# Token-sum stores in the feed-forward, the surplus branch two steps earlier, and feed-forward weight loads ahead of the last outputs

## The chip, the cores and the metric

The kernel runs on one core of one Trainium2 chip, as one launch. The metric is the device time of an execution in microseconds (us). The engines are TensorE (PE, matmul; PEld its weight loads), VectorE (DVE), ScalarE (ACT), GpSimd (POOL) and SyncE (SP, which here issues nearly all DMAs). Each engine runs its own instructions in order and waits for others through semaphores.

## The reference

```python
# retention: 8 batches x 8 heads, 576 positions, head width 64
ret = (q @ k.transpose(0, 1, 3, 2)) / sqrt(64) * Dmat   # Dmat[h,i,j] = gamma_h**(i-j), 0 where j > i
x = (ret @ v) laid out as 4608 tokens x 512
# top-1 mixture of 8 experts
logits = x @ w_gate + modality_bias[modality_id]
e = argmax(logits); gate = softmax(logits)[e]
x = gate * (relu(x @ w1[e]) @ w2[e])                    # 512 -> 1024 -> 512
# dense feed-forward
h = relu(x @ w_in)                                      # 512 -> 2048
out = (h * h) @ w_out                                   # 2048 -> 512
```

All inputs and the output are fp32. The kernel computes each product with fp32 accuracy from a high and a low part of both operands: three matmuls, high by high, high by low and low by high.

## The kernel before, in words

**Stages.** `phase0` computes the retention and the routing. `phase12` (line 664) runs the experts over sorted slots of tokens: a first slot "E", then slots 0 to 8 (`NF` is 8, the last one, 256 tokens wide, the others 512). `phase3` (line 1087) runs the dense feed-forward over nine tiles of 512 tokens, three passes over 3, 3 and 2 blocks of the hidden width. Intermediate data lie in device memory: `yd` the experts' outputs, `sd` the token numbers of the sorted order, `wc` the feed-forward weights in sums and split, `xc` the token sums of a tile, `pd` partial outputs.

**A slot.** Each slot has eight steps f = 0 to 7. A step is `first` (the first product, 12 matmuls per step, relu into hh and hl by ACT and DVE) and `second` (12 matmuls that add to four banks). The first of step f+1 is written ahead of the second of step f. The weights of two steps come as two raw loads `wr` (`wload`, line 400, three buffers) that ACT and DVE split into high and low (lines 149 and 150). At f = 7, `second` copies the slot's result to ye, stores it to yd (line 834) and stores the token numbers to sd (line 835, pieces of 4 bytes).

**Side work of the last slots.** `combos` (lines 745 to 781) reads tile 0 of yd (line 750), makes the seven token sums that the feed-forward's seven-product scheme wants, in tiles x0 to x3 that stay for the feed-forward, and stores each to xc (line 762). `wload2` (line 1008, the load is line 1012) loads one feed-forward weight block, two tiles of 917 KB: w00, w01, w02 are the first product's three blocks, w10, w11, w12 those of the second, each with 0 and 1 for high and low. `extras` (line 922) holds the blocks for surplus tokens under a branch (line 904); with these inputs none is taken, so every engine only jumps over it.

**The order of the feed-forward.** A planner (`Plan`, line 1020) takes all operations of phase 3 with a cost on each engine and what they read and write, and places them in a list schedule by start and due time; the code is emitted in that order. `xprep` (line 1151) loads a tile's yr from yd, makes the seven sums x0 to x3 (two per tile), and stores them to xc. `one` is the first product of a block with its relu and square into z and split into h; `two` is the second product into oe. All DMAs of phase 3 are issued by SP at line 1129, in the planner's order.

Of the kernel before, what the change touches and what calls it, by code (L numbers as in the profile page):

```python
# [88 lines left out]
def kernel(ctx, tc, qT, kT, kN, vN, modT, w_gate, mbias, w1, w2, w_in, w_out,  # L89
# [574 lines left out]
    def phase12():  # L664
        with ExitStack() as c1:
# [79 lines left out]
            def combos():  # L745
                for _ in cs:
                    pass
                yr = cv.tile([P, KD, TS], F32, tag="w", name="eyr")
                tx = cv.tile([P, 2, 256], F32, tag="w", name="etx")
                sp.dma_start(yr, yd[:, 0:TS].rearrange("(c p) t -> p c t", p=P))  # L750
                yield 1
                xs = [cv.tile([P, 2, 2, 2, 256], F32R, tag="w", name=f"x{a}") for a in range(4)]
                b11, b12 = yr[:, 0:2, 0:256], yr[:, 0:2, 256:512]
                b21, b22 = yr[:, 2:4, 0:256], yr[:, 2:4, 256:512]

                def sub(o, a, b):
                    dve.tensor_tensor(out=o, in0=a, in1=b, op=ALU.subtract)

                def put(m, src):
                    t_ = held["x", m] = xs[m // 2][:, m % 2]  # L760
                    split(t_[:, 0], t_[:, 1], src, dve)
                    sp.dma_start(xc[0, m], t_.bitcast(F32).rearrange("p a k t -> p (a k t)"))

                sub(tx, b12, b11)
                put(0, b11)
                yield 1
                put(1, b21)
                yield 1
                sub(b12, b22, b12)
                put(2, b22)  # L770
                yield 1
                sub(b11, b22, tx)
                put(3, tx)
                yield 1
                put(5, b12)
                yield 1
                sub(b21, b21, b11)
                put(4, b11)
                yield 1
                put(6, b21)  # L780
                yield 1
# [28 lines left out]
            def second(u, cols=range(KD)):  # L810
                s, f = u
                wd = width(s)
                hh, hl = HS.pop(u)
                w = W[s, f // 2][1]
                for c in cols:
                    if f == 0:
                        Y[s, c] = new(psY, [P, TS], F32, f"y{c}", f"y{c}")
                    cs = slice(c * P, c * P + P)
                    three(Y[s, c][:, :wd], (w[:, 0, f % 2, cs], w[:, 1, f % 2, cs]), (hh, hl), f == 0, f == 7)
                if f == 7:  # L820
                    if 0 in cols:
                        YE[s] = new(rp, [P, KD, TS], F32, "raw", "ye")
                    ye = YE[s]
                    for c in cols:
                        act.activation(ye[:, c, :wd], Y[s, c][:, :wd], AF.Copy)
                    if 3 not in cols:
                        return
                    ix = XG[s][1]
                    if s == "E":
                        yo, so = yd[:, 0:TS], sd[0:TS]  # L830
                    else:
                        reg = sp.value_load(slots[0:1, 2, s:s + 1], min_val=0, max_val=NT)
                        yo, so = yd[:, bass.ds(reg, wd)], sd[bass.ds(reg, wd)]
                    sp.dma_start(yo.rearrange("(c p) t -> p c t", p=P), ye[:, :, :wd])
                    sp.dma_start(so.rearrange("(j p) -> p j", p=P), ix[:, :wd // P])
# [113 lines left out]
            for i, u in enumerate(us):  # L949
                s, f = u  # L950
                k = seq.index(s)
                nx = seq[k + 1] if k + 1 < len(seq) else None
                if nx is not None and f == (4 if s == "E" else 0):
                    gather(nx)
                if i + 1 < len(us):
                    first(us[i + 1])
                if nx is not None:
                    if s == "E" and f == 6:
                        trans(nx, 0)
                        trans(nx, 1)  # L960
                    elif s != "E" and 3 <= f <= 6:
                        trans(nx, f - 3)
                if u == (NF, 7):
                    wload2(1, 0, wp)
                second(u)
                if s == "E" and f == 6:
                    trans(nx, 2)
                    trans(nx, 3)
                if i == 2:
                    route_c(last)  # L970
                if i == 0:
                    for _ in route_a(last):
                        pass
                elif i == 1:
                    tb = table()
                    next(tb)
                    for _ in route_b(last, dve):
                        next(tb)
                elif i == 2:
                    ws(6, 2, 7)  # L980
                    tab_out()
                    for _ in range(10):
                        next(tb)
                elif i == 3:
                    for _ in tb:
                        pass
                    ws(8, 2, 11)
                else:
                    wl(i + 9)
                    fill(wsg(i + 6, 2 if i < 10 else 1, i + 9), part(cs, 2250))  # L990
                    if i >= 68:
                        run(ex, 3)
                    if i == 73:
                        assert next(cs, 0) == 0 and next(ex, 0) == 0
                        wload2(0, 0, cv)
                if u == (NF, 1):
                    wload2(0, 1, wp)
                if u == (NF, 4):
                    extras()
                if u == (NF, 5):  # L1000
                    wload2(0, 2, wp)
                if i == 6:
                    ext = nc.values_load(slots[0:1, 3, 0:1], min_val=0, max_val=NX)
            assert st["ld"] == st["sp"] == nw
# [82 lines left out]
    def phase3():  # L1087
        with ExitStack() as c2:
            ff = c2.enter_context(tc.tile_pool(name="ff", bufs=1))
            sb = lambda name, shape, dt=F32R: ff.tile(shape, dt, tag=name, name=name)  # L1090
            plan = Plan()
            for j in (1, 2):
                wload2(1, j, wp, False)
            WT = [[[held["w", m, j, x] for x in range(2)] for j in range(3)] for m in range(2)]
            XT = [held["x", m] for m in range(7)]
            HT = [sb(f"h{j}", [P, 2, 7, 256]) for j in range(3)]
# [31 lines left out]
            def dma(o, i, kb, r, w, early=False):  # L1128
                plan.add(m_(kb), lambda e: (pool if early else e).dma_start(o, i), r, w, 2.0)
# [21 lines left out]
            def xprep(n):  # L1151
                p, t = T3[n]
                if n == 0 or T3[n - 1][1] == t:
                    return
                if p:
                    for x in AT1:
                        m = MX[x]
                        dma(XT[m].bitcast(F32).rearrange("p a k t -> p (a k t)"), xc[t, m], 512, [("xc", t, m)],
                            [("x", m, 0), ("x", m, 1)])
                    return  # L1160
                for a in range(2):
                    dma(yr[:, 2 * a:2 * a + 2],
                        yd[2 * a * P:2 * a * P + 2 * P, t * TS:t * TS + TS].rearrange("(c p) t -> p c t", p=P),
                        512, [], [("b", a, 0), ("b", a, 1)])
                b11, b12 = yr[:, 0:2, 0:256], yr[:, 0:2, 256:512]
                b21, b22 = yr[:, 2:4, 0:256], yr[:, 2:4, 256:512]
                k11, k12, k21, k22 = ("b", 0, 0), ("b", 0, 1), ("b", 1, 0), ("b", 1, 1)
                def put(x, src, k):
                    m = MX[x]
                    hilo(XT[m][:, 0], XT[m][:, 1], src, 512, [k], ("x", m, 0), ("x", m, 1))  # L1170
                    dma(xc[t, m], XT[m].bitcast(F32).rearrange("p a k t -> p (a k t)"), 512,
                        [("x", m, 0), ("x", m, 1)], [("xc", t, m)])

                sub = ALU.subtract
                tt(xt, b12, b11, sub, 512, [k12, k11], [("t",)], p_(512))
                tt(b12, b22, b12, sub, 512, [k22, k12], [k12], p_(512))
                put(1, b11, k11)
                tt(b11, b22, xt, sub, 512, [k22, ("t",)], [k11], p_(512))
                put(2, b21, k21)
                tt(b21, b21, b11, sub, 512, [k21, k11], [k21], p_(512))  # L1180
                put(6, b11, k11)
                put(5, xt, ("t",))
                put(7, b12, k12)
                put(4, b21, k21)
                put(3, b22, k22)
# [115 lines left out]
            for n in range(9, len(T3)):  # L1301
                VO.append(VO[-1] if T3[n][1] == T3[n - 1][1] else 1 - VO[-1])
            plan.add([(DMA_, 8.0)], lambda e: None)
            loadw(0, 1, 1)
            for n, (p, t) in enumerate(T3):
                nq = len(PASSES[p])
                order = sorted((7 * q + AT1[x], q, x) for q in range(nq) for x in AT1)
# [53 lines left out]
```

## Time and profile before

| | us |
|---|---|
| median of 3 runs | 1434.08 (1429.42 to 1436.12) |
| the profiled execution's own time | 1428.05 |
| its span in the trace | 1426.3 |
| TensorE busy in the span | 1358.7 (95%) |
| VectorE, ScalarE, GpSimd busy | 1026.4 (72%), 635.8 (45%), 172.6 (12%) |
| mean granted TensorE clock | 0.984 |

The experts end and the feed-forward begins at about 661 us of the span. An entry such as `PE L787 MATMUL bank<-hh,wy` is a TensorE instruction of line 787 that reads hh and wy and writes a PSUM bank; `[4.96 <-ACT hh L803]` says that the engine was idle for 4.96 us before it, and that ACT's writing of hh at line 803 ended this. A `q` behind an engine's name (SPq, DVEq) is its instruction queue. PEclk is the clock that was granted to TensorE, as a share of full speed.

### The profile page before, as it was taken

The numbers are of one execution on the slowest core, as the hardware profiler recorded it, in microseconds if no ns is written. First come the engines' busy times: TensorE is split into PE (matmuls) and PEld (weight loads), VectorE is DVE, ScalarE is ACT, GpSimd is POOL, SyncE is SP. The second block draws the span as 40 slices with busy tenths as digits, with TensorE's granted clock in tenths as the row PEclk, the third lists the DMA queues.
The fourth block names the chain that finished last, engine by engine and source line by source line (L and its number), as shares of the span: only waits on it lengthen the run. The fifth ranks groups of instructions, "written<-read, shape, count | busy, mean of one in ns | idle before, by whom it ended". The sixth has DMA issues, their size and how long they took to land. (4 is left out here: it accounts for less than half of the span.)

```text
span 1426.3 us, 26456 instructions
## 1 busy us (share of the span) xinstructions
PE 1358.7 (95%) x10384; PEld 1251.9 (88%) x10384; DVE 1026.4 (72%) x2004; ACT 635.8 (45%) x1317; POOL 172.6 (12%) x164
## 2 busy tenths in 40 slices
PE   6999998999999999988899999999999999999985
PEld 6898877888788888878899999999999999999984
DVE  2677756887878878553888887767766777688764
ACT  1444543545354454443555555554434444334321
POOL 3222112101110110000211111100000000021112
PEclk9999999999999999998999999999999999999998
DMA  9978256888889888888644455477445564787672
GB/s 341 355 271 296 78 167 229 246 237 254 298 244 269 251 318 229 236 235 272 234 178 178 185 215 194 179 312 265 174 163 195 211 224 184 276 278 274 222 252 102
DMA packets 143733, 332.40 MB, mean 233 GB/s; under 512 B 20208, under 2 KB 54512, under 8 KB 143600
## 3 DMA queue, kind: packets, MB, share of 16 engines
q1 hardware_dynamic: 135520, 310.06, 64.9%
q0 software_dynamic: 5920, 19.40, 3.6%
q8 instruction: 83, 1.36, 0.4%
q10 hardware_dynamic: 2160, 1.17, 0.3%
q14 instruction: 50, 0.41, 0.1%
HBM read 222.57 MB, written 108.02 MB: 232 GB/s over the span
## 5 line engine op out<-in xcount | busy, mean ns | idle before, releaser
L1140 PE MATMUL bank<-w,h 128*128 128x256 f32 x1008 | 284.8, 283 | 9.4 <-DVE h L1241 9.4
L1138 PE MATMUL bank<-w,h 128*128 128x256 f32 x1008 | 283.9, 282 | 7.8 <-DVE oe L1116 7.7
L1138 PE MATMUL bank<-x,w 128*128 128x256 f32 x1008 | 285.8, 284 | 1.4 <-DVE z L1116 0.9
L1139 PE MATMUL bank<-x,w 128*128 128x256 f32 x1008 | 285.7, 283 | 1.5 <-DVE x L1116 1.5
L1140 PE MATMUL bank<-x,w 128*128 128x256 f32 x1008 | 285.4, 283 | 0.1
L1139 PE MATMUL bank<-w,h 128*128 128x256 f32 x1008 | 283.3, 281 | 1.2 <-DMA w<-wc 1.2
L1113 ACT ACTIVATE z<-bank 128x256 f32<-128x256 f32 x288 | 109.1, 380 | 277.2 <-PE bank L1140 258.4
L1140 PEld LDWEIGHTS bank<-w,h 128*128 128x128 f32 x1008 | 190.3, 189 | 12.2 <-DVE h L1241 11.9
L1138 PEld LDWEIGHTS bank<-w,h 128*128 128x128 f32 x1008 | 191.0, 189 | 9.3 <-DVE oe L1116 8.2
L1139 PEld LDWEIGHTS bank<-x,w 128*128 128x128 f32 x1008 | 193.1, 192 | 2.1 <-DVE x L1116 2.1
L1138 PEld LDWEIGHTS bank<-x,w 128*128 128x128 f32 x1008 | 192.7, 191 | 1.8 <-DVE z L1116 1.1
L1140 PEld LDWEIGHTS bank<-x,w 128*128 128x128 f32 x1008 | 193.2, 192 | 0.4 <-DMA w<-wc 0.4
L1139 PEld LDWEIGHTS bank<-w,h 128*128 128x128 f32 x1008 | 190.3, 189 | 1.4 <-DMA w<-wc 1.4
L1240 ACT ACTIVATE h<-z 128x512 fp32r<-128x512 f32 (+2 forms) x270 | 158.1, 599 | 68.4 <-DVE z L1116 46.5
L1241 DVE TENSOR_TENSOR h<-z,h 128x512 fp32r<-128x512 f32 (+2 forms) x270 | 173.8, 672 | 3.7 <-ACT h L1240 3.7
L1116 DVE TENSOR_TENSOR z<-z,bank 128x256 f32<-128x256 f32 x216 | 89.7, 418 | 58.8 <-PE bank L1140 53.4
L787 PE MATMUL bank<-hh,wy 128*128 128x512 f32 (+1 forms) x320 | 127.0, 397 | 5.0 <-ACT hh L803 5.0
L787 PE MATMUL bank<-xh,wx 128*128 128x512 f32 (+1 forms) x320 | 124.5, 389 | 3.4 <-PEq L904 3.4
L788 PE MATMUL bank<-xl,wx 128*128 128x512 f32 (+1 forms) x320 | 124.3, 388 | 1.1 <-DVE xl L743 1.1
L788 PE MATMUL bank<-hl,wy 128*128 128x512 f32 (+1 forms) x320 | 124.4, 389 | 0.7 <-DVE hl L804 0.7
L1116 DVE TENSOR_TENSOR z<-z 128x256 f32<-128x256 f32 x288 | 121.8, 451 | 3.1
L789 PE MATMUL bank<-xh,wx 128*128 128x512 f32 (+1 forms) x320 | 123.9, 387 | 0.0
(168 smaller groups left out, 2223.4 us busy)
## 6 DMA issues: line engine op xcount, KB each, us to landing
x<-xc SPq DMA_DIRECT2D x112, 512.0 KB
wr<-w SPq DMA_DIRECT2D x80, 512.0 KB
xc<-x SPq DMA_DIRECT2D x63, 512.0 KB
w<-wc SPq DMA_DIRECT2D x32, 896.0 KB
wc<-cwh SPq DMA_DIRECT2D x16, 896.0 KB
wc<-cwl SPq DMA_DIRECT2D x16, 896.0 KB
pd<-oe SPq DMA_DIRECT2D x24, 512.0 KB
xd<-xs SPq DMA_DIRECT2D x9, 1024.0 KB
```

The source lines that it names most:

```text
L787: pe.matmul(ps, lh, rh, start=first, stop=False)
L788: pe.matmul(ps, lh, rl, start=False, stop=False)
L789: pe.matmul(ps, ll, rh, start=False, stop=last)
L1113: plan.add(a_(c), lambda e: e.activation(o, i, f), r, w)
L1116: plan.add(engs or d_(c), lambda e: e.tensor_tensor(out=o, in0=a, in1=b, op=op), r, w)
L1138: e.matmul(ps[n], lh, rh, start=first and n == 0, stop=False, skip_group_check=True)
L1139: e.matmul(ps[n], lh, rl, start=False, stop=False, skip_group_check=True)
L1140: e.matmul(ps[n], ll, rh, start=False, stop=True, skip_group_check=True)
L1240: plan.add(a_(c), lambda e: e.activation(h[:, 0, a:b], z[:, a + 1:b + 1], AF.Copy), rs, ks[0])
L1241: plan.add(d_(c), lambda e: e.tensor_tensor(out=h[:, 1, a:b], in0=z[:, a + 1:b + 1], in1=h[:, 0, a:b].bitcast(F32), op=ALU.subtract), rs + ...
```

## The change

The store of each token sum is taken out of `combos`; `xprep` issues those seven stores of tile 0 ahead of tile 1's loads, in an order that the planner chooses. `extras` moves from behind step 4 of the last slot to behind step 2. The load of w02 moves from step 5 to step 3, that of w10 from step 7 to step 4; w11 is loaded at step 5, and w12 inside the `second` of step 7, ahead of the stores to yd and sd. Before, w11 and w12 were loaded by the planner's code.

```diff
@@ combos @@
                     split(t_[:, 0], t_[:, 1], src, dve)
-                    sp.dma_start(xc[0, m], t_.bitcast(F32).rearrange("p a k t -> p (a k t)"))
@@ second, f == 7 @@
                     ix = XG[s][1]
+                    if s == NF:
+                        wload2(1, 2, wp)
                     if s == "E":
@@ the loop over steps @@
-                if u == (NF, 7):
-                    wload2(1, 0, wp)
                 second(u)
...
                 if u == (NF, 1):
                     wload2(0, 1, wp)
-                if u == (NF, 4):
+                if u == (NF, 2):
                     extras()
-                if u == (NF, 5):
-                    wload2(0, 2, wp)
+                for f_, m, j in ((3, 0, 2), (4, 1, 0), (5, 1, 1)):
+                    if u == (NF, f_):
+                        wload2(m, j, wp)
@@ phase3 @@
-            for j in (1, 2):
-                wload2(1, j, wp, False)
@@ xprep @@
+                if n == 1:
+                    for m in range(7):
+                        dma(xc[0, m], XT[m].bitcast(F32).rearrange("p a k t -> p (a k t)"), 512,
+                            [("x", m, 0), ("x", m, 1)], [("xc", 0, m)])
                 for a in range(2):
@@ phase3 @@
-            loadw(0, 1, 1)
             for n, (p, t) in enumerate(T3):
```

On VectorE in the last expert slot the rows ahead of the branch were these (wx and wy are split weight blocks, hl the low part of a step's hidden values):

```order
L804 SCALAR_TENSOR_TENSOR hl_5961<-bank7_91,hh_5960 128x256
L150 TENSOR_TENSOR wy_5976<-wr2_5876,wy_5976 128x1024
L804 SCALAR_TENSOR_TENSOR hl_5992<-bank5_89,hh_5991 128x256
L804 SCALAR_TENSOR_TENSOR hl_6020<-bank6_90,hh_6019 128x256
L904 COMPARE_AND_BRANCH
```

and are now:

```order
L150 TENSOR_TENSOR wx_5930<-wr1_5815,wx_5930 128x1024
L803 SCALAR_TENSOR_TENSOR hl_5954<-bank7_91,hh_5953 128x256
L150 TENSOR_TENSOR wy_5969<-wr2_5869,wy_5969 128x1024
L905 COMPARE_AND_BRANCH
```

Two hl have moved behind the branch, and the split of the last wy stands right ahead of it.

On SyncE at the end of that slot (w020 is the first of the two tiles of w02, and so on) it was:

```order
L1012 DMA w020_9090<-wc_95 128x1792
L1012 DMA w021_9092<-wc_95 128x1792
L1012 DMA w100_9122<-wc_95 128x1792
L1012 DMA w101_9124<-wc_95 128x1792
L832 TENSOR_LOAD slots_100
L832 ISA x2
L834 REGISTER_ALU
L834 DMA yd_93<-ye_9138 128x4x256
L835 REGISTER_ALU
L835 DMA sd_94<-ix_5525 128x2x1
L1129 DMA w110_9163<-wc_95 128x1792
L1129 DMA w111_9164<-wc_95 128x1792
```

and from w101 on it is now:

```order
L1012 DMA w110_9091<-wc_95 128x1792
L1012 DMA w111_9093<-wc_95 128x1792
L1012 DMA w120_9140<-wc_95 128x1792
L1012 DMA w121_9142<-wc_95 128x1792
L833 TENSOR_LOAD slots_100
L833 ISA x2
L835 REGISTER_ALU
L835 DMA yd_93<-ye_9135 128x4x256
L836 REGISTER_ALU
L836 DMA sd_94<-ix_5525 128x2x1
L1127 DMA xc_97<-x0_5726 128x1024
L1127 DMA yr_9170<-yd_93 128x2x512
```

The four loads of w11 and w12 now stand ahead of the stores to yd and sd, and a store to xc stands between these and the first load of yr.

On ScalarE in the first feed-forward tile (z and h of the three blocks, x0 of tile 1, oe the output) the rows were:

```order
L1113 ACTIVATE z2_9172<-bank5_89 128x256
L1121 ACTIVATE z1_9171<-z1_9171 128x256
L1122 ACTIVATE z1_9171<-z1_9171 128x256
L1240 ACTIVATE h2_9169<-z2_9172 128x512
```

and are now:

```order
L1111 ACTIVATE z2_9169<-bank5_89 128x256
L1111 ACTIVATE x0_5726<-yr_9170 128x512
L1119 ACTIVATE z1_9168<-z1_9168 128x256
L1120 ACTIVATE z1_9168<-z1_9168 128x256
L1242 ACTIVATE h2_9166<-z2_9169 128x512
```

The copy of x0 out of yr, which stood behind the first copy to oe, now stands inside the last block's z and h work.

## Rows read from the trace of the kernel before

**Rows 1.** Timeline of TensorE, last expert slot: start, duration, instruction, [idle before, its releaser].

```profile
634.74 0.28 PE L787 MATMUL bank<-xh,wx 128*128 128x256 f32 x1
644.12 0.58 PE L787 MATMUL bank<-hh,wy 128*128 128x256 f32 x1 [4.96 <-ACT hh L803]
645.44 0.58 PE L788 MATMUL bank<-hl,wy 128*128 128x256 f32 x1 [0.74 <-DVE hl L804]
651.57 0.55 PE L787 MATMUL bank<-xh,wx 128*128 128x256 f32 x1 [3.42 <-PEq L904]
661.41 0.28 PE L1138 MATMUL bank<-x,w 128*128 128x256 f32 x1
```

**Rows 2.** Windows; columns: length, busy (count) of PE, PEld, DVE, ACT, POOL, PEclk, DMA share, GB/s.

```profile
632.00:640.00 8.00, 7.16 (x61) 6.95 (x59) 1.65 (x2) 0.46 (x2) 0.00 (x0) 1.00 1.08 149
652.00:657.00 5.00, 5.00 (x25) 5.00 (x25) 0.42 (x1) 0.38 (x1) 0.00 (x0) 0.50 0.57 217
```

**Rows 3.** Timeline of ScalarE, three loads that it waited for.

```profile
411.50 1.06 ACT L149 ACTIVATE wy<-wr 128x1024 fp32r<-128x1024 f32 x1 [3.43 <-DMA wr<-w]
614.97 0.63 ACT L149 ACTIVATE x<-eyr 128x512 fp32r<-128x512 f32 x1 [8.03 <-DMA eyr<-yd]
642.74 1.06 ACT L149 ACTIVATE wy<-wr 128x1024 fp32r<-128x1024 f32 x1 [8.84 <-DMA wr<-w]
```

**Rows 4.** Timeline of SyncE's issues; the duration is that of the issue.

```profile
396.25 0.40 SPq L834 DMA_DIRECT2D yd<-ye  x1
608.64 0.51 SPq L750 DMA_DIRECT2D eyr<-yd  x1
616.35 0.34 SPq L762 DMA_DIRECT2D xc<-x  x1
628.01 0.40 SPq L834 DMA_DIRECT2D yd<-ye  x1
629.88 0.89 SPq L400 DMA_DIRECT2D wr<-w  x1
630.82 1.23 SPq L1012 DMA_DIRECT2D w<-wc  x1
662.02 0.40 SPq L834 DMA_DIRECT2D yd<-ye  x1
672.85 0.39 SPq L1129 DMA_DIRECT2D yr<-yd  x1
```

**Rows 5.** Line 904; columns: engine, operation, count, ns min/median/max, first to last start.

```profile
L904 SPq EVENT_SEMAPHORE  x9: 17/17/17, 645.4 to 652.9; - x9
L904 SPq COMPARE_BRANCH  x1: 53/53/53, 633.7 to 633.7; - x1
L904 DVEq COMPARE_BRANCH  x1: 72/72/72, 644.4 to 644.4; - x1
L904 DVEq EVENT_SEMAPHORE  x1: 21/21/21, 649.8 to 649.8; - x1
```

**Rows 6.** Timeline of VectorE, last expert weight block.

```profile
643.83 1.23 DVE L150 TENSOR_TENSOR wy<-wr,wy 128x1024 fp32r<-128x1024 f32 x1 [9.47 <-ACT wy L149]
```

**Rows 7.** Transfers, 652 to 690 us in 40 slices of 0.95 us.

```profile
GB/s 17 0 219 355 430 400 415 430 415 430 423 372 357 210 204 34 78 46 60 53 99 75 98 355 438 407 445 402 407 423 386 411 373 144 24 0 0 203 349 280
```

**Rows 8.** Timeline of TensorE, first feed-forward tile.

```profile
683.11 0.39 PE L1139 MATMUL bank<-w,h 128*128 128x256 f32 x1 [1.23 <-DMA w<-wc]
```

**Rows 9.** Waits, 680 to 700 us; columns: who, for what, total us, times, longest.

```profile
PE bank L1139 <- DVE x L1116: 1.5, 3, 0.7
```

**Rows 10.** Waits, 705 to 722 us, second feed-forward tile.

```profile
PE bank L1140 <- DVE h L1241: 1.5, 2, 0.8
PE bank L1138 <- DVE z L1116: 0.9, 1, 0.9
```

**Rows 11.** Timeline of ScalarE, first feed-forward tile.

```profile
675.57 0.41 ACT L1121 ACTIVATE z<-z 128x256 f32<-128x256 f32 x1
685.65 0.63 ACT L1113 ACTIVATE x<-yr 128x512 fp32r<-128x512 f32 x1 [0.52 <-DMA yr<-yd]
```

## The prediction

> **What bounds the kernel now.** TensorE is busy for 95% of the span, so a microsecond counts only if it opens or closes a gap of TensorE or lowers its clock. I read the timeline of TensorE's gaps first, then for each gap the engine that ended it, then SyncE's issues and the transfer rate beneath them. The reader is to see three things.
>
> First, the last expert slot holds the costliest stops near the change [rows 1]. TensorE waits 4.96 us for ScalarE's hh, 0.74 us for VectorE's hl and 3.42 us at the branch of line 904, 9.12 us in all. From 634.74 to 661.41 us it runs nine groups of twelve matmuls. At full clock 61 matmuls take 7.16 us [rows 2], 0.117 each, so nine groups are worth 12.7 us; the remaining 26.67 - 9.12 - 12.7 = 4.8 us are the clock. The granted clock is 0.50, the lower level (1.2 GHz), after the stop at the branch [rows 2]; the five groups behind it take 661.41 - 651.57 = 9.84 us where full clock would give 7.0, a price of 2.8 us for one stop.
>
> Second, the first wait comes from a load. ScalarE stood for 8.84 us until the last expert weight load arrived at 642.74 [rows 3]; that load was issued at 629.88, right behind the slot-7 stores of 628.01 [rows 4].
>
> Third, at the end of the slot the transfers go in SyncE's order: four w loads, yd and sd, four w loads, yr [rows 4]. They run at some 410 GB/s except for about 9 us, from 664 to 673, at 34 to 200 GB/s [rows 7], where yd and sd are next in that order; SyncE could issue yr, which waits for yd, at 672.85 [rows 4].
>
> **The change part by part.**
>
> *The branch two steps up.* In the old order two more first-half groups and two second-half groups stand ahead of the branch, and the load's wait falls inside them. In the new order TensorE reaches the branch when it would start the group of 634.74, and its first matmul behind it waits for VectorE, whose last instruction ahead of the branch is the split of that last weight block. So the two waits no longer share anything: load, split, crossing, restart come one behind the other. The split started 1.1 us after the load's arrival [rows 6], 643.8 with the old load time; VectorE's crossing took 649.8 - 644.4 = 5.4 us [rows 5]; with its branch read half a microsecond or so earlier than before, the restart is at about 649.3. TensorE's own crossing is hidden in this wait, and so is SyncE's, which ends no earlier than before, as it waits for the same loads w000 to w011 (645.4 to 652.9, [rows 5]). TensorE stands 649.3 - 634.74 = 14.6 us in place of 9.12. The clock falls once in place of twice: 2.8 us in place of 4.8. The slot ends at 649.3 + 12.7 + 2.8 = 664.8, **3.4 us later** than 661.41. Bounds: -4 us if the load comes as early as the lone load of 608.64, whose reader went on at 614.97, 6.3 us [rows 3, 4]; +10 us if VectorE's crossing takes as long as SyncE's, 645.4 - 633.7 = 11.7 us [rows 5]. I take VectorE's own.
>
> *The token-sum stores.* Seven stores of 512 KB leave the stretch from 616.35 on [rows 4] and come back in the first feed-forward tile, where two of them stand ahead of the halves of yr. Does the last expert load get earlier? It lies behind yd and sd, and it came 14.7 us after yd's issue here; after the yd store of 396.25 the next load was used at 411.50, 15.25 us, with no xc store near it [rows 3, 4]. So I cost the removal at nothing. The bound on the gain is the 6.3 us above, in full: 14.7 - 6.3 = 8 us earlier.
>
> *Feed-forward weights ahead of the outputs.* Now eight w loads are issued behind the crossing, from 653 on; the last waits until the slot's last matmul has read its buffer, 664.8, and yd stands behind it on SyncE. In [rows 7] the rate of about 410 GB/s makes 2.2 us of each 917 KB load, so eight take 17.9 us: ring clear at 653.0 + 0.9 + 17.9 = 671.8. A slot end up to 7 us later than mine would not move this, which is why the sum depends little on the term before. Then yd and sd, 9 to 9.5 us by the slow stretch of [rows 7]: yd has landed at about 681.3, where in the old order it had at 672.85. Then xc and the first half of yr, 512 KB each, 2.6 us and about 1 us of issue and arrival: **yr is there at about 685.0**, the second half near 687.5. In the old order ScalarE had yr at 685.65 [rows 11], so yr itself is hardly later; what differs is who stands behind it.
>
> *The new place of the token sums.* ScalarE's copy of x0 out of yr now stands ahead of the Relu, Square and h copy of the first tile's last block (the order below the diff shows it), and ScalarE goes in order. From yr: x0 0.63, Relu and Square 0.41 each [rows 11], the h copy 0.6 and VectorE's part of h 0.65, both estimates from x0, which has the same 128x512: 685.0 + 2.7 = 687.7 for the first second-half group of that block. It stands 156 matmuls, 18.7 us at 0.12, and half a microsecond of stall (an estimate from [rows 9]) into the tile; the old schedule passes this point at 661.41 + 19.2 = 680.7, the new would at 684.0 and waits for 3.6 us. So TensorE is **7.0 us late** here, slot included. Behind it I put 1.2 us of small stalls as x0 and x1 now go between and 2.3 us of clock, since a stop of 3.42 us cost 2.8 [rows 1, 2]. What the old tile lost afterwards goes away: 1.23 us for the last w load [rows 8], covered by the earlier issue, and 1.5 us for VectorE's x [rows 9]. Together 7.0 + 1.2 + 2.3 - 2.7 = +7.8 us. Of the second tile's stalls 1.5 and 0.9 us [rows 10] go, because tile 1's sums are already made: **-2.4**. The rest of the feed-forward keeps its order but for a slip of one or two tiles; zero, with 2 us either way.
>
> Sum: +5.4 us, call it +5. On the profiled run's own time of 1428.05 that is 1433; this run is 6 us under the median of 1434.08, its range being 1429.42 to 1436.12, so against the median I forecast **1439 us**.
>
> The sd store writes pieces of 4 bytes. The Trainium skill (DMA: Bandwidth & Descriptors, Specifications) says that pieces under 512 B fall below line rate, since the engine reads, modifies and writes. The trace agrees: 34 to 200 GB/s with the two stores in flight [rows 7], and 149 GB/s at a DMA share of 1.08 between 632 and 640 [rows 2]. It speaks against the change: by it the slow stretch belongs to sd, not to the xc stores, so taking these out buys no earlier load, and yr stands behind the stretch without other work to fill it. By the rule the sum stays at +5; were the xc stores the cause, it would be rival C's.
>
> **The rivals.**
>
> *A, slower than before: yr comes 1 to 2 us later and nothing is given back.* The place is ScalarE's x0 in the first tile. It decides once yr's first half comes later than about 686, as when the second xc store goes ahead of it or the stores of 512 KB halve its rate. Price: 7.8 + 1.5 us without the 2.4 given back, +9.3, 1443 us. For it: each microsecond of yr is a microsecond of TensorE from there. Against it: two free microseconds stand in the estimate of arrival, and old stalls [rows 10] were of the kind that earlier sums remove.
>
> *B: no stop at yr.* If yd and sd pass in 5 us rather than 9, as they would if the slow stretch were partly the w loads' own, yr is there at 681 and its chain ends at 683.6, in time. What is left is 3.4 + 1.2 - 2.7 - 2.4 = -0.5 us, 1434 us. Against it stands the length of the stretch in [rows 7].
>
> *C, a gain: the xc stores delayed the last weight load.* Then the load comes 6 us earlier, the restart at 643, the slot ends 3 us earlier than before, yr is there before it is asked for, and the tile's stalls go too: -3 and up to -2.4, with the stretch up to -4, 1430 us; the outer end is 1427. For it: seven stores were issued in the 10 us before yd. Against it: 396.25.
>
> **How the numbers follow.** Forecast 0.40 (1436 to 1442), A 0.26, B 0.21, C 0.13. A measurement of this kernel can tell about 0.5%, 7.2 us, from no change. A's outer two thirds and the forecast's upper tail with VectorE's long crossing pass +7.2: 0.29. Of C the outer half passes -7.2 with the spread of the median, 0.07. The rest, 0.64, is within. The range reaches from C's 1428 to 1448, A with 5 us more for the crossing and the spread.
>
> **What would show it.** One TensorE gap of about 14.6 us up to 649, released by VectorE or the branch; a slot end near 665; yd's landing near 681 with SyncE's yr behind it; ScalarE idle for yr near 685, and a TensorE gap of some 3 to 4 us behind it at the lower clock. It is wrong if the load of 642.7 moves by more than 2 us, if TensorE passes the first tile without a stop, or if the sum lies in tiles that I cost at zero.

## The result and the profile after

The changed kernel takes 1440.34 us at the median (15 runs, 1436.02 to 1449.35), the kernel before 1434.05 in the same number (1420.21 to 1438.49). The ratio is 1.0073, 95% interval 1.0052 to 1.0094: slower, by some 7 to 13 us. The means of the two are 10.0 us apart, the medians 6.3. The forecast was 1439. The span of the profiled execution is 1437.5 us, where it was 1426.3, at a mean clock of 0.979.

The rows of TensorE that answer to [rows 1] (timeline: start, duration, instruction, idle before and its releaser):

```profile
651.20 0.58 PE L786 MATMUL bank<-xh,wx 128*128 128x256 f32 x1 [13.37 <-DVEq L905]
665.57 0.28 PE L1136 MATMUL bank<-x,w 128*128 128x256 f32 x1
691.57 0.58 PE L1136 MATMUL bank<-w,h 128*128 128x256 f32 x1 [7.20 <-ACT h L1242]
694.28 0.58 PE L1138 MATMUL bank<-w,h 128*128 128x256 f32 x1 [1.92 <-DVE h L1243]
```

The three stops of the slot are one of 13.37 us, ended by VectorE's queue at the branch. A stop of 7.20 us stands in the first feed-forward tile, where none was over 1.3 us. Its cause is in ScalarE's timeline and in SyncE's, which answer to [rows 3, 4, 11]:

```profile
644.33 1.06 ACT L149 ACTIVATE wy<-wr 128x1024 fp32r<-128x1024 f32 x1 [7.50 <-DMA wr<-w]
689.61 0.63 ACT L1111 ACTIVATE x<-yr 128x512 fp32r<-128x512 f32 x1 [9.78 <-DMA yr<-yd]
```

```profile
630.60 0.40 SPq L835 DMA_DIRECT2D yd<-ye  x1
666.93 0.40 SPq L835 DMA_DIRECT2D yd<-ye  x1
668.75 0.46 SPq L1127 DMA_DIRECT2D xc<-x  x1
685.38 0.38 SPq L1127 DMA_DIRECT2D yr<-yd  x1
```

yd is issued at 666.93, the load of yr, which waits for its landing, 18.45 us later; before, it was 10.83 us. ScalarE idles 9.78 us for yr. The branch (the view of [rows 5]: count, ns min/median/max, first to last start):

```profile
L905 PEldq COMPARE_BRANCH  x1: 13082/13082/13082, 635.6 to 635.6; - x1
L905 DVEq COMPARE_BRANCH  x1: 72/72/72, 645.4 to 645.4; - x1
L905 DVEq EVENT_SEMAPHORE  x1: 21/21/21, 651.1 to 651.1; - x1
```

VectorE reads its branch as the split of the last weight block begins and is over it 5.7 us later; TensorE starts 0.1 us after that. In all fourteen profiles of this document VectorE's crossing takes 5.4 to 5.8 us. TensorE's own, read at 635.6, lasted 13.1 us, 5.9 before; it ended at 648.7, still inside the stop. Why it took longer is not shown. The clock in two windows (columns as in [rows 2]; here and below `...` stands for lines left out):

```profile
651.00:656.00 5.00, 4.80 (x28) 4.81 (x29) 0.42 (x1) 0.38 (x1) 0.00 (x0) 0.65 0.42 136
...
692.00:698.00 6.00, 4.08 (x19) 3.78 (x19) 5.96 (x7) 2.96 (x7) 4.49 (x3) 0.50 1.03 422
```

And the transfer rate from 655 to 693 us, in 40 slices of 0.95 us, as in [rows 7]:

```profile
GB/s 174 309 415 423 415 423 423 423 423 423 430 430 440 415 408 423 423 355 257 252 341 339 243 24 69 17 18 49 52 5 22 4 4 58 239 418 410 397 431 423
```

The eight loads run at some 420 GB/s until 671; from 677 to 685 the rate is 4 to 69 GB/s, with yd, sd and one xc store in the queue.

**Where the time stands.** Both traces hold the same 10,384 matmuls, so the n-th of one can be set beside the n-th of the other. I use three: the last ahead of the changed kernel's stop (number 4,228), the first of the feed-forward (4,337) and number 9,001, early in the third pass, behind all that the change touches. The kernels in the table other than before and changed are told under the experiments. "Slot" is the time from the first to the second, "feed-forward" from the second to the third. What lies ahead of 4,228 already differed by 2.93 us in the changed kernel's profile; 2.65 us of this are there by 320 us of the span, long before any code that was changed runs.

| kernel | slot, us | feed-forward, us | sum against before | timed ratio, 95% interval |
|---|---|---|---|---|
| before | 26.79 | 572.47 | 0 | 1 |
| before_again | 27.52 | 571.72 | 0.0 | (one time) |
| changed | 28.02 | 579.29 | +8.1 | 1.0073 (1.0052 to 1.0094) |
| e1_branch_back | 23.68 | 586.13 | +10.6 | 1.0061 (1.0035 to 1.0087) |
| e2_xc_back | 27.77 | 578.15 | +6.7 | 1.0065 (1.0025 to 1.0105) |
| e4_w12_behind | 29.10 | 576.76 | +6.6 | 1.0073 (1.0045 to 1.0101) |
| e5_late_x0 | 26.45 | 573.69 | +0.9 | 0.9994 (0.9961 to 1.0027) |
| e6_sd_early | 23.23 | 576.00 | 0.0 | 1.0018 (0.9994 to 1.0043) |
| e7_branch_only | 29.34 | 571.19 | +1.3 | 1.0044 (1.0013 to 1.0075) |
| e8_both | 23.21 | 573.70 | -2.4 | 1.0027 (1.0002 to 1.0052) |
| e10_stores_only | 24.57 | 572.60 | -2.1 | 0.9988 (0.9953 to 1.0022) |
| b_sd_early | 26.36 | 571.83 | -1.1 | 1.0001 (0.9975 to 1.0027) |
| e9_sd_late | 21.18 | 574.39 | -3.7 | 0.9964 (0.9936 to 0.9992) |
| e11_stores_sd | 21.60 | 570.12 | -7.5 | 0.9951 (0.9925 to 0.9978) |

Slot and feed-forward rest on one profile in each row. The two profiles of before differ by 0.7 us in the slot and by as much, the other way, in the feed-forward. The changed kernel, e4 and e5 have the same code up to the restart, and their slots lie between 26.45 and 29.10 us. So a single slot tells a difference of 3 us and not one of 1 us.

### The profile page after: what moved, and what is told of

Same layout as the page of the kernel before. It is cut to its first block, busy times and chain, and to the rows that moved or that the text cites. A ratio compares the mean times of both kernels' runs of the same rounds, so it can differ in the third digit from the quotient of the medians.

```text
span 1437.5 us, 26460 instructions
## 1 busy us (share of the span) xinstructions
PE 1358.3 (94%) x10384; PEld 1252.2 (87%) x10384; DVE 1027.7 (71%) x2007; ACT 633.9 (44%) x1311; POOL 171.3 (12%) x164
## 5 line engine op out<-in xcount | busy, mean ns | idle before, releaser
L1138 PE MATMUL bank<-w,h 128*128 128x256 f32 x1008 | 285.0, 283 | 11.5 <-DVE h L1243 11.4
L1138 PEld LDWEIGHTS bank<-w,h 128*128 128x128 f32 x1008 | 190.6, 189 | 14.6 <-DVE h L1243 14.5
L786 PE MATMUL bank<-xh,wx 128*128 128x512 f32 (+1 forms) x320 | 124.8, 390 | 13.4 <-DVEq L905 13.4
```

What stands on the lines that cost most here:

```text
L786: pe.matmul(ps, lh, rh, start=first, stop=False)
L1138: e.matmul(ps[n], ll, rh, start=False, stop=True, skip_group_check=True)
```

## The experiments

**e1_branch_back.**

```diff
-                if u == (NF, 2):
+                if u == (NF, 4):
                     extras()
```

> The changed kernel with extras() back behind step 4. Theory (the first feed-forward tile is paid by ScalarE's x0 waiting for yr, whose time is set by the transfers): the stop before the slot's restart splits into two again and the slot ends about 1.5 us earlier, but yr comes at the same time, within 1 us, counted from the slot-7 stores; the gap of TensorE in the first tile grows from 7.2 to about 8.5 us and the total stays within 1 us of the changed kernel's, some 7 to 9 us over the kernel before. Rival (the moved branch is the cost): 4 us or more of the loss go.

Timeline of TensorE:

```profile
649.58 0.55 PE L786 MATMUL bank<-xh,wx 128*128 128x256 f32 x1 [4.65 <-PEq L905]
690.21 0.58 PE L1136 MATMUL bank<-w,h 128*128 128x256 f32 x1 [10.57 <-ACT h L1242]
```

ScalarE:

```profile
688.26 0.63 ACT L1111 ACTIVATE x<-yr 128x512 fp32r<-128x512 f32 x1 [13.15 <-DMA yr<-yd]
```

The slot is 4.3 us shorter than the changed kernel's, more than the 1.5 expected, and all of it is lost again: yr is used 60.0 us behind the issue of slot 7's yd (628.27), in the changed kernel 59.0, and TensorE's stop grows from 7.20 to 10.57 us. The sum is 2.5 us worse, where "within 1 us" was expected. So the rival, that the moved branch is the cost, fails here: the slot's length does not reach the end while yr gates the tile.

**e2_xc_back.** The seven stores return to `combos` and leave `xprep`.

```diff
                     split(t_[:, 0], t_[:, 1], src, dve)
+                    sp.dma_start(xc[0, m], t_.bitcast(F32).rearrange("p a k t -> p (a k t)"))
...
-                if n == 1:
-                    for m in range(7):
-                        dma(xc[0, m], ...)
```

> The changed kernel with the seven xc stores of tile 0 back in combos; the planner then puts two x0 copies and x1 ahead of the last block's z and h on ScalarE. Theory: the last expert weight load comes about 1 us later again (14.7 us behind yd's issue, not 13.7); yr, no longer behind an xc store, comes 1 to 2.5 us earlier behind yd's landing, but three copies (1.9 us) stand ahead of h2, so the gap in the first tile stays at 6 to 8 us; total within 2 us of the changed kernel's. Rival (the xc stores in the ring are the cost of the first tile): the gap falls under 3 us and 5 us or more go.

```profile
692.35 0.58 PE L1137 MATMUL bank<-w,h 128*128 128x256 f32 x1 [6.59 <-ACT h L1239]
695.72 0.58 PE L1139 MATMUL bank<-w,h 128*128 128x256 f32 x1 [2.58 <-DVE h L1240]
```

The stop is still 6.59 us (TensorE's timeline), and the sum 1.4 us better. The xc stores among the yr loads are not what costs the first tile. The load came 13.3 us behind yd's issue, not the 14.7 expected with the stores back, and yr was used 4.6 us behind yd's landing, in the changed kernel 4.2, where 1 to 2.5 us less were expected.

**e4_w12_behind.** The same loads, behind the outputs.

```diff
-                    if s == NF:
-                        wload2(1, 2, wp)
...
                     sp.dma_start(so.rearrange("(j p) -> p j", p=P), ix[:, :wd // P])
+                    if s == NF:
+                        wload2(1, 2, wp)
```

> The changed kernel with the two loads of w12 behind the yd and sd stores; ScalarE's order is unchanged, x0 ahead of h2. Theory (weights ahead of the outputs make yd late): yd is issued as early as before but meets a ring two loads shorter, so it lands 2 to 4 us earlier (about 681 to 683 in place of 685.4), the two w12 loads (4.4 us) then stand ahead of yr, so yr comes at about the same time or 1 to 2 us later, and the first tile's gap stays at 6 to 9 us. Rival (only the order on SyncE counts): yr comes 4 us earlier and the gap falls to about 3 us.

SyncE's timeline, then TensorE's:

```profile
666.42 0.40 SPq L833 DMA_DIRECT2D yd<-ye  x1
679.04 0.39 SPq L1127 DMA_DIRECT2D yr<-yd  x1
```

```profile
689.77 0.58 PE L1136 MATMUL bank<-w,h 128*128 128x256 f32 x1 [5.17 <-ACT h L1242]
```

The load of yr could be issued 6 us sooner behind yd (12.62 us, not 18.45), where 2 to 4 us were expected. The two w12 loads then stood ahead of yr, and the stop is 5.17 us, a little under the 6 to 9 expected and far from the rival's 3. As the theory has it: moving two loads round yd mostly trades one wait for another.

**e5_late_x0.** One number of the planner; the transfers at the slot's end keep their order.

```diff
-            plan.add([(DMA_, 8.0)], lambda e: None)
+            plan.add([(DMA_, 24.0)], lambda e: None)
```

> The changed kernel with one number of the planner changed, its initial charge on the DMA queue from 8 to 24 us, so that it expects yr later: x0 of tile 1 comes behind the last block's z and h and the first oe copies on ScalarE; the transfers at the slot's end keep their order. Theory (ScalarE blocked at x0 holds TensorE): yr comes at the same time as in the changed kernel, and yet the 7.2 us gap goes and the clock stays up there; the total falls by 6 to 9 us, to within 2 us of the kernel before in the traces. Rival (yr's lateness itself or the clock or the branch is the cost, whoever waits): a gap of 5 us or more appears elsewhere in the first two tiles and the total falls by less than 3 us.

```profile
647.56 0.58 PE L786 MATMUL bank<-xh,wx 128*128 128x256 f32 x1 [11.45 <-DVEq L905]
697.99 0.39 PE L1136 MATMUL bank<-x,w 128*128 128x256 f32 x1 [1.45 <-DVE z L1114]
718.27 0.38 PE L1138 MATMUL bank<-w,h 128*128 128x256 f32 x1 [2.37 <-DVE h L1243]
```

```profile
682.91 0.38 SPq L1127 DMA_DIRECT2D yr<-yd  x1
```

The load of yr is issued 54.0 us behind slot 7's yd (628.90), in the changed kernel 54.8: no earlier to speak of. Yet the stop of 7.20 us is gone, two of 1.45 and 2.37 us are left, the sum falls from +8.1 to +0.9, and the timed ratio from 1.0073 to 0.9994. Of the 7.2 us, 5.6 lie in the feed-forward; the other 1.6 lie in the slot, whose code is the same. The planner's number moves other work as well, but TensorE's own order is the same up to matmul 4,498, and the stop of 7.20 us stood at number 4,493. This is the run that settles the cause: ScalarE, in order, stood at x0 with the last block's z and h behind it. The same edit between e1_branch_back and e8_both takes 12.4 us from the feed-forward (586.13 to 573.70).

Where the planner's wrong estimate comes from can be read in the code. The change took the loads of w11 and w12 out of the planner's code (`loadw(0, 1, 1)`), four loads of 917 KB, which it had charged at 320 GB/s to its DMA queue: 11.5 us in all. Its starting charge stayed at 8 us, so it expected yr earlier. The runs fit: in e10_stores_only, where these loads are still in the plan, x0 comes behind the last block's z and h; in e2_xc_back, where they are not, it comes ahead, although the stores are back.

**e6_sd_early.** The changed kernel; the sd store leaves `second` (surplus slots keep it there) and is issued from the loop over steps, with its own read of the slot's place.

```diff
-                    sp.dma_start(so.rearrange("(j p) -> p j", p=P), ix[:, :wd // P])
+                    if s != "E" and s > NF:
+                        sp.dma_start(so.rearrange("(j p) -> p j", p=P), ix[:, :wd // P])
...
+            def sdput(s):
...
+                sp.dma_start(so.rearrange("(j p) -> p j", p=P), XG[s][1][:, :wd // P])
...
+                if f == 5:
+                    sdput(s if s == "E" else (s if s < NF - 1 else NF)) if s != NF else None
+                if u == (NF - 1, 1):
+                    sdput(NF - 1)
```

> The changed kernel with the sd store of every slot taken out of the slot's end and issued some steps earlier (the last slot's at step 5 of slot 7, slot 7's at its step 1). Theory (the 4-byte pieces of sd make the slow stretch that yd shares): yd lands 5 to 8 us earlier behind the eight w loads (in the changed kernel 8.5 us behind the last of these), yr comes as much earlier, the 7.2 us gap in the first tile falls under 2 us; the last expert weight load comes 2 to 5 us earlier behind slot 7's yd (13.7 us in the changed kernel); in all 8 to 11 us less than the changed kernel. Rival (the yd store is slow by itself, with its 1 KB rows, or by its completion): yd still takes 8 us or more behind the last w load, the gap stays at 6 us or more, and the total at +0.5% or more over the kernel before.

```profile
646.05 0.58 PE L786 MATMUL bank<-xh,wx 128*128 128x256 f32 x1 [8.68 <-DVEq L915]
687.86 0.58 PE L1152 MATMUL bank<-w,h 128*128 128x256 f32 x1 [2.87 <-DVE h L1257]
```

```profile
639.05 1.06 ACT L149 ACTIVATE wy<-wr 128x1024 fp32r<-128x1024 f32 x1 [2.67 <-DMA wr<-w]
```

The last expert load is used 8.9 us behind yd's issue (630.15), in the changed kernel 13.7, and the slot's stop is 8.68 us, not 13.37. In the first tile ScalarE still idles 5.4 us for the two halves of yr, but TensorE's longest stop is 2.87 us, a little more than expected, and the one ahead of it that was 7.20 is 0.79. Of the changed kernel's 8.1 us nothing is left in the sum, in spite of its order on ScalarE: the slot is 3.6 us shorter than before, the feed-forward 3.5 us longer. So stores of 1 and 2 KB of token numbers, in 4-byte pieces, held the ring. That it is the size of the pieces which makes them slow was not tried.

**e7_branch_only.** The kernel before, with:

```diff
-                if u == (NF, 4):
+                if u == (NF, 2):
                     extras()
```

> The kernel before with extras() moved from step 4 to step 2 and nothing else. Theory by the changed kernel's trace: one stop of 13 to 14 us in place of 4.96, 0.74 and 3.42, one spell at the lower clock; counted from the last matmul ahead of the stop the slot ends 1 to 3.4 us later than in the kernel before; the first tile's stalls are as in the kernel before; total +1 to +3.5 us. Rival (the branch costs as much as e1_branch_back's slot makes it look against the changed kernel, 4.3 us): +4 us or more. Rival (two stops made into one give a gain): 0 or below.

```profile
648.28 0.58 PE L787 MATMUL bank<-xh,wx 128*128 128x256 f32 x1 [13.87 <-DVEq L904]
663.48 0.28 PE L1138 MATMUL bank<-x,w 128*128 128x256 f32 x1
```

The stop is 13.87 us, the slot 1.8 to 2.6 us longer than in the two profiles of before, the sum +1.3, as the theory has it, though one profile does not tell so little for certain. The timed ratio, 1.0044, is larger than the sum explains (6 us, its interval reaching from 2 to 11); where the rest would lie I did not find, and by the times alone the rival of +4 us or more is not excluded.

**before_again.** No edit.

> The kernel before, unchanged, profiled a second time, to see how far a stage of the same kernel moves from one execution to the next. Expected: the stop at the last slot and the first tile's stalls within 1 us of the first profile; the part ahead of 600 us and the part behind 1300 us anywhere within 5 us. If the slot itself moves by 3 us, the difference between the slots of e1_branch_back and of the kernel before says nothing about the xc stores.

```profile
1313.92 0.38 PE L1138 MATMUL bank<-w,h 128*128 128x256 f32 x1 [2.29 <-DVE oe L1116]
...
1337.21 0.58 PE L1138 MATMUL bank<-w,h 128*128 128x256 f32 x1 [3.11 <-DVE yr L1116]
...
1364.36 0.58 PE L1138 MATMUL bank<-w,h 128*128 128x256 f32 x1 [4.36 <-DVE oe L1116]
```

From matmul 4,228 to 9,001 the two executions agree to 0.02 us, in part by luck, as slot and feed-forward differ by 0.7 us each way. Behind 1300 us they do not agree: three stops here, 9.76 us together, a single one of 6.66 us in the first profile, and two spells of the lower clock where the first profile has one. From number 9,001 to the end this profile loses 6.7 us, more than the 5 expected, and ends 5.7 us later. Sums in the table stop at 9,001 for this reason.

**e8_both.** e1_branch_back and e5_late_x0 together, on the changed kernel:

```diff
-                if u == (NF, 2):
+                if u == (NF, 4):
                     extras()
...
-            plan.add([(DMA_, 8.0)], lambda e: None)
+            plan.add([(DMA_, 24.0)], lambda e: None)
```

> The changed kernel with extras() back behind step 4 and the planner's initial DMA charge at 24 us, so that the x0 copies come late. Theory: the slot's end of e1_branch_back (3.1 us earlier than in the kernel before) and the first tile of e5_late_x0 (1.7 us of stalls less than before, perhaps some 2 us more as the weights of the last block are now asked for earlier) add up: -2 to -5 us against the kernel before, ratio 0.996 to 0.999. Rival (e1's early slot end is taken back whenever the first tile has to wait for yr, in whatever order): a gap of 3 us or more in the first two tiles, and a ratio of 1.000 or above.

The gains add up in the trace (slot 23.21, sum -2.4 us), but the timed ratio is 1.0027, above the range that I gave and in the rival's. The stop of 3 us or more that the rival wants is not there: the longest in the first two tiles is 1.89 us. The sum is not the whole of the time; in the two profiles of before the stage behind 1300 us moved by more than that.

**e10_stores_only.** The kernel before with the two edits to the xc stores alone:

```diff
-                    sp.dma_start(xc[0, m], t_.bitcast(F32).rearrange("p a k t -> p (a k t)"))
...
+                if n == 1:
+                    for m in range(7):
+                        dma(xc[0, m], ...)
```

> The kernel before with the xc stores of tile 0 moved into the feed-forward and nothing else; the planner puts x0 behind the last block's z and h here. Theory (the stores lengthen the way of the last expert weight load by 2 to 3 us, as e1_branch_back and e8_both make it look): that load comes about 12 us behind slot 7's yd, not 14.7, and the slot ends 2.5 to 3.5 us earlier than in the two profiles of the kernel before; in the first tile no gap over 2 us; -1 to -4 us from the last matmul ahead of the stop to the end of pass 0. Rival (the stores cost the load nothing and the slot of e1 is another effect of the earlier weight loads): load and slot within 1 us of the kernel before.

```profile
641.40 0.39 PE L786 MATMUL bank<-hh,wy 128*128 128x256 f32 x1 [3.33 <-ACT hh L802]
...
677.23 0.56 PE L1138 MATMUL bank<-w,h 128*128 128x256 f32 x1 [2.33 <-DMA w<-wc]
```

The first stop is 3.33 us, 4.96 and (in the second profile) 5.80 before; the slot 2.2 to 3.0 us shorter, the sum -2.1. The load came 13.4 us behind yd's issue, not the 12 expected, and the first tile's stop of 2.33 us is over the 2 expected. The ratio, 0.9988, can't be told from 1.

**b_sd_early.** The kernel before with the diff of e6_sd_early.

> The kernel before with the sd stores issued some steps earlier, as in e6_sd_early, and nothing else. Theory (the sd store holds up the last weight load by 4 to 5 us): the load comes about 10 us behind yd, the first stop of 4.96 us falls to 0 to 1 us, the slot ends 4 to 6 us earlier; ratio 0.996 to 0.999. Rival (another load or the crossing ends the stop in its place): the slot ends less than 2 us earlier and the ratio is 0.999 to 1.001.

```profile
639.30 0.38 PE L787 MATMUL bank<-hh,wy 128*128 128x256 f32 x1 [3.49 <-ACT hh L803]
```

The theory failed here, and the rival's numbers came: the load still landed 14.1 us behind yd's issue, the first stop was 3.49 us, the slot 26.36, the ratio 1.0001. But what ended the stop was the same load, not another one or the crossing. With the xc stores in the ring, taking sd out buys next to nothing.

**e9_sd_late.** The diffs of e8_both and e6_sd_early on the changed kernel.

> e8_both (the changed kernel, branch back at step 4, x0 late) with the sd stores early. Theory: sd's 4 to 5 us come on top in the slot, and yr is there before it is asked for, so nothing waits in the first tile: -5 to -8 us against the kernel before up to the end of pass 0, ratio 0.994 to 0.998. Rival (the branch's own crossing is next and takes the gain): the slot gains less than 1 us over e8_both, ratio 1.000 to 1.003.

```profile
641.14 0.55 PE L786 MATMUL bank<-xh,wx 128*128 128x256 f32 x1 [5.06 <-PEq L915]
707.66 0.38 PE L1152 MATMUL bank<-w,h 128*128 128x256 f32 x1 [2.35 <-DVE h L1257]
```

The slot falls to 21.18 us, 2.0 less than in e8_both, so the rival fails, and the ratio to 0.9964 (0.9936 to 0.9992). The sum of -3.7 is short of the -5 to -8 expected. The feed-forward takes 574.39 us; stops of 1.45 and 2.35 us stand there at the same matmuls as the two of e5_late_x0, the other run with a late x0.

**e11_stores_sd.** The diffs of e10_stores_only and e6_sd_early on the kernel before; branch, weight loads and planner as in the kernel before.

> The kernel before with two edits: the xc stores moved into the feed-forward and the sd stores early; branch and weight loads as before. Theory: the gains of e10_stores_only and b_sd_early in the slot add up until the stop for the load is gone (4.96 us and a part of the clock's 4.8), the 3.42 us of the crossing stay: -5 to -8 us up to the end of pass 0, ratio 0.994 to 0.998. Rival (the two gains are the same 5 us of one wait): no better than the better of the two by more than 1 us.

```profile
637.41 0.39 PE L787 MATMUL bank<-hl,wy 128*128 128x256 f32 x1 [0.62 <-DVE hl L803]
643.95 0.55 PE L786 MATMUL bank<-xh,wx 128*128 128x256 f32 x1 [4.97 <-PEq L913]
674.11 0.39 PE L1153 MATMUL bank<-w,h 128*128 128x256 f32 x1 [1.36 <-DVE h L1258]
```

```profile
GB/s 106 226 392 385 347 415 377 423 408 438 339 332 274 309 364 324 332 392 423 423 430 355 324 363 405 410 427 386 410 425 416 427 423 418 418 185 289 293 0 43
```

The second fence is the transfer rate from 645 to 683 us: the slow stretch is gone, nothing between the loads is under 274 GB/s until the queue empties at 678. The load came 9.5 us behind yd's issue; its stop is gone but for 0.62 us, and the crossing's 4.97 us is what is left of the slot's stops. The median is 1424.88 us beside 1430.59 for before, 0.9951 (0.9925 to 0.9978): faster than both kernels. Alone the two edits gave 2.1 and 1.1 us, together 7.5, of which 5.2 lie in the slot: either backlog was enough to keep the load late, which is why neither alone showed its price. All fourteen profiles bear this out. The load came 13.3 to 14.9 us behind yd's issue with both backlogs, 11.9 to 14.0 with sd alone, 14.2 with the xc stores alone (one profile), and 8.9 to 9.5 with neither.

## Why the prediction was right, and where it was not

*Forecast and size.* Slower by a third of a per cent was forecast; the ratio says 0.73%, the medians 0.44%. The forecast had +5.4 us from the branch on, the trace has +8.1. Of the stated cases the truth lies between the forecast and rival A, whose condition (the first half of yr later than about 686) came true: 689.61 less the 2.93 us that the whole stage was late is 686.7. So the mechanism, ScalarE at x0 waiting for yr with TensorE behind it, was right and the price too low. That the forecast of 1439 stands so near the median of 1440.34 is in part luck: the slot was put 2.2 us too dear, the stop in the first tile 3.6 us too cheap, and 1.2 us too much was given back, which leaves 2.6 us. By the means, 10.0 us apart, it would stand further off.

*Slot: +3.4 forecast.* It was +1.2 in the changed kernel and +1.8 to +2.6 for the branch alone. The stop was 13.37 us, not 14.6, as the load came 13.7 us behind yd, not 14.7; the restart was ended by VectorE's crossing, as forecast. The other mis-sized term is the clock: 2.8 us were put down, but by the trace's record of the granted clock the lower level ended at 654.55, 3.35 us behind the restart. Up to there matmuls are 0.21 us apart and not 0.117: 3.35 x (1 - 0.117 / 0.213) = 1.5 us. The window of 0.65 shows it beside the 0.50 of before. The prediction's "once in place of twice" is misread too: before, the clock fell once, at 643.89, just ahead of the end of the first stop, and stayed at the lower level across the one at the branch until 657.54.

*Stores: nothing forecast.* Wrong by some 2 to 3 us in the slot, in rival C's direction: with the branch at step 4 and sd in its place the slots are 23.2 to 24.6 us without the stores (e1, e8, e10), 26.8 and 27.5 with them. The timed ratio of e10_stores_only can't show so little. The argument from the store at 396.25, that the load is as late without xc stores, was sound as far as it went (b_sd_early and e10 show each backlog to be enough), but did not see that with both gone the load comes at 9.5 us (e11_stores_sd).

*Weights ahead: yd at 681.3.* It landed at 685.4; less the 2.93 us this is 682.4. The stretch behind the last w load took 8.5 us (676.9 to 685.4 by the landing times of the two), 9 to 9.5 were put down; the eight loads were through at 673.9 by the same reckoning, 2.1 us later than put down. That sd makes this stretch, as the Trainium skill's rule on pieces under 512 B (DMA: Bandwidth & Descriptors, Specifications) led the prediction to say, is now shown as far as the store goes, though not for the size of its pieces: without sd, yd landed 1.6 us behind the last w load in e6_sd_early, and 1.5 to 1.9 us in the other three runs without it. Rival B, that yd and sd pass sooner, fell with it.

*First tile: a stop of 3.6 us.* It was 7.20. Two terms make the difference: the tile was asked for 2.2 us sooner than forecast (a slot of +1.2, not +3.4), and yr came 1.7 us later (686.7, not 685.0). "yr itself is hardly later" was a misreading: 685.65 in [rows 11] is the copy of yr's second half, the first half's started at 684.51. The forecast's remark that a slot's length does not matter while yr gates is what e1_branch_back shows. Behind the stop, 1.92 us for VectorE's h and the lower clock up to 698.92 cost about as much as put down (1.2 and 2.3); the old waits of [rows 8, 9] went, as forecast.

*Second tile: -2.4.* Only 1.2 us came back. The waits of [rows 10] did not go but were replaced, by 0.81 and 1.13 us for VectorE's h, where 2.4 us stood before. This is the other half of rival A. Behind it, up to number 9,001, the changed kernel stays some 11 us late, 2.9 of them from ahead of the slot: the rest of the order was rightly costed at nothing.

## What to carry to other kernels

A list scheduler that does not know when a transfer lands puts its consumer where the model has it ready; on an engine that goes in order, everything behind that consumer then waits, and here one number of the model (8 to 24 us) was worth 5.6 us of the feed-forward in one pair of kernels and 12.4 in another. Whoever takes transfers out of such a scheduler's account must put their time back into its start. Before a store is moved, ask which of several backlogs in the ring keeps the next load late: each may look nearly free alone, and their sum is seen only when all are gone. A store of small pieces whose data are known early belongs where no load is waited for.

## What was not expected of the hardware

The same kernel's two executions agree to 0.02 us over 600 us, with 0.7 us either way inside, but differ by 6.7 us in the last 120 us, where TensorE's stops fell in three places of 2.29, 3.11 and 4.36 us rather than one of 6.66. The lower clock level lasted 3.35 us behind one restart and 6 us behind another with a shorter stop (13.37 and 3.42 us), so that the longer stop had the cheaper restart: at 640.9, three microseconds into the 13.37 us stop, the granted clock had already fallen, while before it fell only at 643.89. With a 1 KB store of 4-byte pieces in the ring the rate stayed at 4 to 69 GB/s for some 8 us; without it, in e6_sd_early, it was under 200 GB/s there for less than 4 us.
